# A second layer's up-projections by Strassen's seven block products, with weight operands kept in DRAM

## The chip, the cores and the metric

The program runs on one core of one Trainium2 chip. The metric is device time in microseconds, the median of several executions. TensorE (PE) multiplies matrices into PSUM, VectorE (DVE), ScalarE (ACT) and GpSimd (POOL) work element by element, and SyncE (SP) issues most DMAs. Weights are held as float32r pairs: a high part and a low part, so that one exact product needs three matmuls.

## The reference, cut to what matters

Linear attention is followed by two gated layers on 2304 tokens (4 batches of 576). The weights and q, k, v arrive as 64-bit floats.

```
x = attention(q, k, v)                     # 2304 x 512
g = x @ w_gate;  val = x @ w_val           # 512 -> 1536
x = (g * sigmoid(g) * val) @ w_out         # layer 1, 1536 -> 512
a = x @ w_a;     b = x @ w_b               # layer 2
out = (a * b) @ w_out2
```

## The kernel before, in words

Tokens are in four blocks of 512 (one for each batch) and a rest block of 256 (the last 64 tokens of each batch). `order` runs layer 1 on blocks 0, 1, 2, rest, 3 and then layer 2 on blocks 0 to 3 and the rest. In a block a loop runs over 12 tiles f of 128 hidden columns. `ups` (L739, `up` L757) multiplies both up-projection weights with x: for each matrix 3 precision passes by 4 chunks of the 512 input columns, so 24 matmuls of 128x512 in two PSUM banks (`gv0`, `gv1`). `gated` (L772) forms the gate on ACT, multiplies on DVE and splits the result into a high part (ACT) and a low part (DVE). `down` (L784) multiplies it with the tile's output weights, 12 matmuls into four accumulators `acc0` to `acc3`, one tile behind `ups`.

Weights are converted on the chip. `convert` (L327) loads the 64-bit words through SP (L351, L356), builds a float32 on ACT and DVE (L380 to L401) and splits it (L406, L298) into the tile's buffer `w0` to `w11` in SBUF. Layer 2 uses the same twelve buffers: its tile f is converted when the last block of layer 1 has used that buffer (`convert_tile(1, f)`; the loads are held by `not_before` until that block has begun). The attention of batches 2 and 3 (`attend`, L440) runs beside layer 1 and uses the staging buffers `wr0`, `wr1`, `a0`, `a1` too.

The order of instructions on every engine is made ahead of time by the class `Plan`. Each operation has a cost in microseconds, and some have a due time: `main["at"]` counts the matmuls' time from `FIRST` and adds `BESIDE` per block for attention. Due times run backward along the dependences; `order` (L117) then goes forward and gives each engine the ready operation with the earliest due time. `pair` (L295) may put an operation on VectorE or on GpSimd; `split` (L303) is a high part on ACT and a low part by `pair`. On the chip each engine runs its list in order and waits by semaphores.

Of the kernel before, what the change touches and what calls it, by code (L numbers as in the profile page):

```python
# [30 lines left out]
class Plan:  # L31
# [20 lines left out]
    def add(self, engine, cost, fn, reads=(), writes=(), due=None, after=(), table=None, nbytes=0, other=None,  # L52
            port=None, hold=()):
        n = len(self.ops)
        deps, order, allocs = set(), set(after) | set(hold), []
        for access, write in [(a, False) for a in reads] + [(a, True) for a in writes]:
            buf, part = access if isinstance(access, tuple) else (access, None)
            if not buf.users:
                if isinstance(buf.tag, tuple):
                    allocs.append(buf)  # L60
                else:
                    if buf.tag in self.last:
                        deps.update(self.last[buf.tag].users)
                    else:
                        buf.free = True
                    self.last[buf.tag] = buf
            elif buf.users[0] != n and not buf.free:
                order.add(buf.users[0])
            if not buf.users or buf.users[-1] != n:
                buf.users.append(n)  # L70
            for key, (last, readers) in buf.seen.items():
                if part is None or key is None or key == part:
                    if last is not None:
                        deps.add(last)
                    if write:
# [142 lines left out]
def kernel(  # L218
# [60 lines left out]
    plan = Plan()  # L279
    add = plan.add  # L280

    def act_us(n):
        return 0.18 + n / 1200

    def dve_us(n, rate=1):
        return 0.15 + n / 960 / rate

    def pool_us(n, streams=2):
        return (0, 0.14 + n / 1100, 0.15 + n / 449, 0.18 + n / 590)[streams]
# [5 lines left out]
    def pair(n, out, x, y, op, reads, writes, either=True, port=True):  # L295

        def run(engine):
            engine.tensor_tensor(out=out(), in0=x(), in1=y(), op=op)  # L298

        add("vector", dve_us(n), lambda: run(nc.vector), reads, writes,  # L300
            other=("gpsimd", pool_us(n), lambda: run(nc.gpsimd), True) if either else None, port=port)

    def split(hi, lo, src, n, hi_key, lo_key, src_key, psum=False):  # L303
        add("scalar", act_us(n), lambda: nc.scalar.copy(out=hi(), in_=src()), [src_key], [hi_key])  # L304
        pair(n, lo, src, lambda: hi().bitcast(F32), ALU.subtract, [src_key, hi_key], [lo_key], not psum, not psum)

    def dma(fn, nbytes, reads, writes, due=None, after=(), issue=0.475, queue="sync", hold=()):
        return add(queue, issue, fn, reads, writes, due=due, nbytes=nbytes, after=after, hold=hold)
# [15 lines left out]
    TOP = 122880.0  # L324
# [85 lines left out]
    def convert_tile(l, f):  # L410
        runs, raw = [(h, [0, 1, 2], [h]) for h in range(2)], None
        if l == 0 and f <= AHEAD:
            raw = Buf(wp, [P, 2, 3, WH, 2], U32, f"w{f + NF - KD - AHEAD - 1}", f"wr{l}_{f}")
            list(convert(l, f, runs, raw))
        else:
            for run in runs:
                list(convert(l, f, [run]))


    def rest(h):  # L420
# [313 lines left out]
    def product(cost, fn, reads, writes):  # L734
        n = add("tensor", cost, fn, reads, writes, due=main["at"], after=main["last"])
        main["at"] += cost
        main["last"] = (n,)
# [63 lines left out]
    def finish(l, i, acc):  # L801
        n = widths[i]
        m = n if l == 0 else DM
        for o, ps in enumerate(acc):
            ob = Buf(op, [P, 512], F32, ("ob0", "ob1"), f"ob{l}_{i}_{o}")

            def copy(engine, fn, us, cols, ob=ob, ps=ps):
                add(engine, us(m), lambda: fn(out=ob()[:, cols], in_=ps()[:, cols]), [ps], [(ob, cols.start)])  # L808

            if (l, i) == (1, B):  # L810
                copy("scalar", nc.scalar.copy, act_us, slice(0, m // 2))
                copy("vector", nc.vector.tensor_copy, dve_us, slice(m // 2, m))
            elif o % 2 == 0:
                copy("scalar", nc.scalar.copy, act_us, slice(0, m))
            else:
                copy("vector", nc.vector.tensor_copy, dve_us, slice(0, m))
            if l == 0:
                dma(lambda ob=ob, o=o: nc.sync.dma_start(out=xd[1][i]()[:, o, :], in_=ob()[:, 0:n]),
                    P * n * 4, [ob], [(xd[1][i], o)], due=main["at"] + 10)
            else:  # L820
                if i < B:
                    rows = [(slice(0, P), out[i * S:i * S + SM, :].rearrange("(p r) e -> p r e", r=R)[:, o, :])]
                else:
                    nb = P // SL
                    rows = [(slice(h * SL, (h + 1) * SL), out[(o * nb + h) * S + SM:(o * nb + h + 1) * S, :])
                            for h in range(nb)]
                for at, row in rows:
                    dma(lambda ob=ob, at=at, row=row: nc.sync.dma_start(out=row, in_=ob()[at, :]),
                        P * DM * 4 // len(rows), [ob], [], due=main["at"] + 10)


    order = [(0, i) for i in (*range(B - 1), B, B - 1)] + [(1, i) for i in range(B + 1)]
    FIRST = 28.0
    BLOCK = NF * 3 * 3 * KD * SM / 2400 * 1.0625
    BESIDE = 11.0

# [25 lines left out]
            list(attend(1, g, None, FIRST + BLOCK * (g + 0.8) / KD))  # L862
    for b in range(2, B):
        for g in range(KD):
            list(attend(b, g, None, FIRST + (BLOCK + BESIDE) * (b - 1) + BLOCK * (g + 0.4) / KD))

    main["at"] = FIRST
    for j, (l, i) in enumerate(order):
        if (l, i) == (1, 0):
            not_before.extend(begun)  # L870
            for f in range(NF):
                convert_tile(1, f)
        acc = [Buf(pa, [P, 512], F32, f"acc{o}", f"acc{l}_{i}_{o}")
               for o in range(KD if l == 0 else widths[i] // P)]
        x = xhl
        before = None
        for f in range(NF):
            ga, gb = ups(l, i, f, x)
            if (l, i, f) == (0, B - 1, 0):
                begun = main["last"]  # L880
            h = gated(l, i, f, ga, gb)
            if before:
                down(l, i, f - 1, before, acc)
            before = h
            if j < B - 1:
                main["at"] += BESIDE / NF
        if j + 1 < len(order):
            xhl = next_x(*order[j + 1])
        down(l, i, NF - 1, before, acc)
        finish(l, i, acc)  # L890

    with tc.manual_schedule():
        plan.emit()
# [30 lines left out]
```

## Time and profile before

| | us |
|---|---|
| median of 3 runs | 992.24 (991.45 to 992.66) |
| span of the profiled execution | 989.2 |
| its own whole time | not listed on the page |
| PE busy | 955.1 (97%), 4616 matmuls |
| DVE busy | 417.3 (42%) |
| ACT busy | 402.8 (41%) |
| POOL busy | 104.5 (11%) |
| moved by DMA | 74.19 MB, mean 75 GB/s |

The span runs from the first to the last instruction. Layer 1 fills it from about 40 to 538 us, layer 2 from 538 to 984. In the table of groups the duration of a matmul includes its way through the array, which overlaps with the next; the time from one matmul to the next is read from the chain of waits.

### The profile page before, as it was taken

The numbers are of one execution on the slowest core, as the hardware profiler recorded it, in microseconds if no ns is written. First come the engines' busy times: TensorE is split into PE (matmuls) and PEld (weight loads), VectorE is DVE, ScalarE is ACT, GpSimd is POOL, SyncE is SP. The second block draws the span as 40 slices with busy tenths as digits, with TensorE's granted clock in tenths as the row PEclk, the third lists the DMA queues.
The fourth block names the chain that finished last, engine by engine and source line by source line (L and its number), as shares of the span: only waits on it lengthen the run. The fifth ranks groups of instructions, "written<-read, shape, count | busy, mean of one in ns | idle before, by whom it ended". The sixth has DMA issues, their size and how long they took to land.

```text
span 989.2 us, 12151 instructions
## 1 busy us (share of the span) xinstructions
PE 955.1 (97%) x4616; PEld 794.2 (80%) x4616; DVE 417.3 (42%) x708; ACT 402.8 (41%) x780; POOL 104.5 (11%) x158
## 2 busy tenths in 40 slices
PE   4789889999999999999999999999999999999997
PEld 3578678888888888998888888888888888888897
DVE  7998985323333332126777782221122112111211
ACT  4888986544544542125555551211121112111211
POOL 5613211000000000001112220000000000000000
PEclk9999999999999999999999999999999999999999
DMA  9935543111211113015445530200020001000100
GB/s 266 289 93 166 173 137 105 49 48 49 91 45 47 48 49 108 11 48 172 132 128 163 178 96 1 64 21 1 1 67 20 1 1 64 1 1 1 43 1 22
DMA packets 77138, 74.19 MB, mean 75 GB/s; under 512 B 29976, under 2 KB 64280, under 8 KB 76184
## 3 DMA queue, kind: packets, MB, share of 16 engines
q1 hardware_dynamic: 71416, 69.36, 22.8%
q10 hardware_dynamic: 5664, 4.07, 1.3%
q8 instruction: 36, 0.59, 0.3%
q14 instruction: 22, 0.18, 0.1%
HBM read 60.29 MB, written 13.11 MB: 74 GB/s over the span
## 4 chain that ended last, share of the span: by engine, by line
PE 91%; DMA 3%; DVE 2%; ACT 1%; SPq 1%; issue 1%; POOL 0%; DVEq 0%; ACTq 0%; POOLq 0%
PE u L765 58%; PE acc L795 15%; PE acc L792 14%; PE xt L699 1%; PE kv L638 1%; DMA ut<-in_q_dram 1%; DMA wr<-in_moe_w_out_dram 1%; DMA wr<-in_moe_w_gate_dram 1%; DMA wr<-in_moe_w_val_dram 0%; DMA x<-xq 0%; SPq L526 0%; PE qt L686 0%; ACT wr L385 0%; SPq L351 0%; DMA ut<-in_k_dram 0%
## 5 line engine op out<-in xcount | busy, mean ns | idle before, releaser
L765 PE MATMUL u<-xhl,w 128*128 128x512 f32 (+1 forms) x2856 | 618.7, 371 | 3.5 <-DVE h L298 1.6
L765 PEld LDWEIGHTS u<-xhl,w 128*128 128x128 f32 x2856 | 496.2, 188 | 98.0 <-issue 3.4
L779 DVE TENSOR_TENSOR u<-s,u 128x512 f32<-128x512 f32 (+1 forms) x120 | 77.1, 642 | 402.8 <-PE u L765 377.9
L776 ACT ACTIVATE s<-u 128x512 f32<-128x512 f32 (+1 forms) x120 | 66.6, 555 | 270.2 <-PE u L765 269.9
L792 PE MATMUL acc<-h,w 128*128 128x512 f32 (+1 forms) x720 | 164.5, 376 | 1.2 <-DVE ob L808 1.0
L795 PE MATMUL acc<-w,h 128*128 128x512 f32 x648 | 157.4, 392 | 0.0
L792 PEld LDWEIGHTS acc<-h,w 128*128 128x128 f32 x720 | 124.1, 188 | 28.1 <-issue 1.9
L795 PEld LDWEIGHTS acc<-w,h 128*128 128x128 f32 x648 | 120.9, 188 | 25.6
L304 ACT CAST h<-u 128x512 fp32r<-128x512 f32 (+1 forms) x120 | 65.0, 542 | 185.6 <-DVE u L779 182.8
L298 DVE TENSOR_TENSOR h<-u,h 128x512 fp32r<-128x512 f32 (+1 forms) x120 | 76.4, 636 | 52.1 <-ACT h L304 51.9
L396 DVE SCALAR_TENSOR_TENSOR a<-wr,a 128x768 uint32<-128x768 uint32 (+2 forms) x45 | 51.2, 1137 | 0.8
L406 ACT CAST w<-a 128x768 fp32r<-128x768 f32 (+2 forms) x45 | 39.3, 874 | 17.5 <-DVE a L401 13.1
L298 POOL TENSOR_TENSOR xhl<-xraw,xhl 128x512 fp32r<-128x512 f32 (+1 forms) x6 | 7.3, 1219 | 346.4 <-ACT xhl L304 249.6
L385 ACT ACTIVATE wr<-wr 128x768 uint32<-128x768 uint32 (+2 forms) x45 | 43.0, 957 | 1.4 <-DMA wr<-in_moe_w_out_dram 1.4
L776 ACT ACT_TABLE_LOAD x24 | 30.8, 1283 | 30.6 <-PE u L765 30.5
L380 ACT ACTIVATE a<-wr 128x768 f32<-128x768 f32 (+2 forms) x35 | 33.4, 954 | 14.5 <-DMA wr<-in_moe_w_out_dram 8.1
L401 POOL TENSOR_TENSOR a<-a,wr 128x768 uint32<-128x768 uint32 (+1 forms) x12 | 23.0, 1916 | 148.7 <-DVE a L396 106.6
L401 DVE CUSTOM_DVE_ANT_0 a<-wr,a 128x1536 uint16<-128x1536 uint16 (+1 forms) x33 | 34.7, 1052 | 1.7
L298 POOL TENSOR_TENSOR w<-a,w 128x768 fp32r<-128x768 f32 (+1 forms) x13 | 25.9, 1989 | 82.5 <-ACT w L406 82.5
L298 DVE TENSOR_TENSOR w<-a,w 128x768 fp32r<-128x768 f32 (+2 forms) x32 | 33.1, 1044 | 2.8 <-ACT w L406 2.7
L387 DVE TENSOR_SCALAR a<-a 128x768 f32<-128x768 f32 (+2 forms) x45 | 28.5, 634 | 6.0 <-ACT a L380 5.6
L390 DVE TENSOR_SCALAR a<-a 128x768 uint32<-128x768 uint32 (+2 forms) x45 | 26.7, 594 | 0.8
(107 smaller groups left out, 469.8 us busy)
## 6 DMA issues: line engine op xcount, KB each, us to landing
wr<-in_moe_w_out_dram SPq DMA_DIRECT2D x46, 256.0 KB, 3.7
xraw<-x SPq DMA_DIRECT2D x7, 1024.0 KB
wr<-in_moe_w_a_dram SPq DMA_DIRECT2D x24, 256.0 KB, 3.7
wr<-in_moe_w_b_dram SPq DMA_DIRECT2D x24, 256.0 KB, 3.1
wr<-in_moe_w_gate_dram SPq DMA_DIRECT2D x22, 256.0 KB, 5.2
wr<-in_moe_w_val_dram SPq DMA_DIRECT2D x22, 256.0 KB, 4.3
x<-ob SPq DMA_DIRECT2D x16, 256.0 KB, 2.5
out_dram<-ob SPq DMA_DIRECT2D x16, 256.0 KB, 3.6
```

Source lines behind the costliest of these rows:

```text
L298: engine.tensor_tensor(out=out(), in0=x(), in1=y(), op=op)
L304: add("scalar", act_us(n), lambda: nc.scalar.copy(out=hi(), in_=src()), [src_key], [hi_key])
L380: add("scalar", act_us(e) + 0.08, lambda rows=rows, halves=halves: nc.scalar.activation(out=a(halves).bitcast(F32), in_=rows()[..., 1].bit ...
L385: add("scalar", act_us(e) + 0.08, lambda rows=rows: nc.scalar.activation(out=rows()[..., 0], in_=rows()[..., 0], func=AF.Copy, scale=2.0 * ...
L396: add("vector", dve_us(e), lambda rows=rows, halves=halves: nc.vector.scalar_tensor_tensor(out=a(halves), in0=rows()[..., 1], scalar=0xC00 ...
L401: engine.tensor_tensor(out=a(halves), in0=a(halves), in1=rows()[..., 0], op=ALU.add)
L406: add("scalar", act_us(size), lambda: nc.scalar.copy(out=part(0), in_=a().bitcast(F32)), every, his)
L765: nc.tensor.matmul(ps()[:, 0:n], lhsT=wv[:, c, :], rhs=x()[:, xs, c, 0:n], start=(a == 0 and c == 0), stop=(a == 2 and c == KD - 1))
L776: add("scalar", act_us(n), lambda: nc.scalar.activation(out=s()[:, 0:n], in_=ga()[:, 0:n], func=AF.Silu if l == 0 else AF.Copy), [ga], [s] ...
L779: add("vector", dve_us(n), lambda: nc.vector.tensor_tensor(out=gb()[:, 0:n], in0=s()[:, 0:n], in1=gb()[:, 0:n], op=ALU.mult), [s, gb], [gb])
L792: nc.tensor.matmul(ps()[:, 0:n], lhsT=w()[:, 4 + ws, o * P:(o + 1) * P], rhs=h()[:, hs, 0:n], start=begin, stop=end)
L795: nc.tensor.matmul(ps(), lhsT=h()[:, hs, o * P:(o + 1) * P], rhs=w()[:, 4 + ws, :], start=begin, stop=end)
```

## The change

Layer 2 is rewritten for the four full blocks. Two blocks of 512 tokens are taken together (a half), and two tiles f (a pair, 256 hidden columns of each matrix). The product of x (512 input columns by 2 blocks) with a pair is a product of 2 by 2 blocks: the input halves h, the token blocks t and the tiles i. It is done by seven products instead of eight, in Winograd's form: four sums of the weights (`t1` to `t4`), four sums of x (`parts`), and seven sums of products (`begin`, `middle`, `end`). One product, `one(m, o)`, is 6 matmuls for matrix m.

The weights of layer 2 are converted by `convert_pair` during layer 1, after the attention of batch 3 (`pair_buf["after"]`). The eight blocks b11 ... t4 of a pair and its output weights are split and stored in DRAM (`wd`). In layer 2 each of 12 steps (2 halves by 6 pairs) loads seven operands into a ring of nine units of 512 KB (in the freed buffers w5 to w8), the output weights into a double buffer, and in the second half b12 for the rest block.

Products go through four PSUM banks (`gv0`, `gv1`, `at0`, `at1`), three for each matrix. The output is no longer gathered in PSUM over all tiles: each step's 8 (or 10) output chunks of 6 matmuls are added into `SUMS` in SBUF. A step's chunks run at the end of the next step. The rest block is done in the second half's steps (`rest_up`). In the due times of layer 1, attention units now follow each other at `EACH` = 22 us and the blocks have other shares of `BESIDE`.

```diff
 def split(hi, lo, src, n, hi_key, lo_key, src_key, psum=False):
+    src_keys = src_key if isinstance(src_key, list) else [src_key]
 ...
+NP = NF // 2
+wd = [Buf(dp, [P, 10, 1024], F32, f"wd{j}", f"wd{j}") for j in range(NP)]
+def convert_pair(j, m):
+    for i in range(2):
+        ...
+        dma(get, P * 2 * WH * 8, [], [LOW, HIGH], issue=0.95 if m < 2 else 0.475, after=pair_buf["after"])
+        ... # abs, scale, clamp, shift, merge, add: 512 columns each
+    def keep(i, h, to):
+        ...
+        split(hi, lo, lambda: a(i)[:, h], WH, ...)
+        ...
+        dma(put, P * 2 * WH * 4, [(key[0], ("s", 0)), (key[0], ("s", 1))], [(wd[j], ...)])
+    if m < 2:
+        ... # keep 4 blocks, 4 subtractions of 256 columns, keep 4 sums
+    else:
+        ... # keep 4 blocks
 ...
-order = [(0, i) for i in (*range(B - 1), B, B - 1)] + [(1, i) for i in range(B + 1)]
+order = [(0, i) for i in (*range(B - 1), B, B - 1)]
+EACH = 22.0
 ...
-        list(attend(b, g, None, FIRST + (BLOCK + BESIDE) * (b - 1) + BLOCK * (g + 0.4) / KD))
+        before = len(plan.ops)
+        list(attend(b, g, None, FIRST + BLOCK + BESIDE + EACH * ((b - 2) * KD + g + 0.4)))
+pair_buf["after"] = tuple(range(before, len(plan.ops)))
 ...
-    if (l, i) == (1, 0):
-        not_before.extend(begun)
-        for f in range(NF):
-            convert_tile(1, f)
 ...
+        if (j, f) == (1, 0):
+            ...
+            for n in range(NP):
+                for m in range(3):
+                    convert_pair(n, m)
 ...
-        if j < B - 1:
-            main["at"] += BESIDE / NF
+        main["at"] += (BESIDE, 2 * BESIDE, BESIDE, 5, 0)[j] / NF
 ...
+PART = 1024
+RING = 9
+BANKS = ("gv0", "gv1", "at0", "at1")
+blocks = [(0, 1), (2, 3)]
+def parts(s):
+    ... # load the halves of two blocks: RAW[0..3]; halve = split of 1024 columns
+    halve(0, 0)
+    halve(5, 3)
+    less(3, 2, 3, ALU.add)
+    less(2, 0, 2)
+    less(0, 3, 0)
+    halve(1, 0)
+    halve(2, 3)
+    halve(3, 1)
+    less(1, 1, 0)
+    halve(4, 2)
+    halve(6, 1)
+def step(s, j):
+    n = s * NP + j
+    w = [unit(14 + (7 * n + o) % RING) for o in range(7)]
+    wo = outs_w[n % 2]
+    for o in range(7):
+        get_w(w[o], j, o)
+    for i in range(2):
+        get_w(wo[i], j, 8 + i)
+    if s:
+        get_w(b12, j, 7)
+    def one(m, o, ps, first):
+        ...
+            for a, (ws, xs) in enumerate(((1, 0), (0, 1), (0, 0))):
+                for c in range(2):
+                    nc.tensor.matmul(ps(), lhsT=wv(o)[:, m, ws, c, :], rhs=..., start=first and a == 0 and c == 0, ...)
+    def begin(m):
+        one(m, 0, p[m][0], True)
+        copy(t[0], p[m][0])
+    def middle(m):
+        one(m, 1, p[m][1], True)
+        plus(t[1], p[m][1], t[0])
+        one(m, 2, p[m][2], True)
+        one(m, 3, p[m][0], False)
+        if m == 0:
+            copy(A[3], p[m][0])
+        else:
+            plus(A[3], p[m][0], A[3], ALU.mult)
+            later.append(lambda: halve(0, 0, A[3]))
+        one(m, 4, p[m][1], False)
+        plus(t[2], p[m][1], t[0])
+        plus(t[2], p[m][2], t[2])
+        if m:
+            times(t[2], A[2])
+            later.append(lambda: halve(1, 1, t[2]))
+    def end(m, which):
+        ... # which 0: product 5 into p[m][1], then t[0]; which 1: product 6 into p[m][2], then t[1]
+    def rest_up(i):
+        ... # 2 x 12 matmuls of 256 columns, gate, split later
+    def out_chunk(k):
+        ... # 6 matmuls of 512 columns into acc{k % 4}, then SUMS[k] += (copy for the first pair)
 ...
+for s in range(2):
+    parts(s)
+    if s:
+        rest_parts()
+    for j in range(NP):
+        begin, middle, end, rest_up, chunks = step(s, j)
+        begin(0)
+        middle(0)
+        begin(1)
+        end(0, 0)
+        end(0, 1)
+        middle(1)
+        for which in range(2):
+            if left:
+                left.pop(0)()
+            end(1, which)
+        for i in range(2 * s):
+            rest_up(i)
+        for c in left:
+            c()
+        for halve in later:
+            halve()
+        later.clear()
+        left = chunks
+    if s == 0:
+        for c in left[:-2]:
+            c()
+        left = left[-2:]
+for c in left:
+    c()
```

## Rows read from the trace of the kernel before

**Rows 1.** Cores: span and mean granted TensorE clock.
```profile
core 0: 989.2 us, clock 0.996
```
**Rows 2.** Page, chain that ended last: shares of the span by engine.
```profile
PE 91%; DMA 3%; DVE 2%; ACT 1%; SPq 1%; issue 1%; POOL 0%; DVEq 0%; ACTq 0%; POOLq 0%
```
**Rows 3.** Stretches: rest block and block 3 of layer 1, a layer 2 block.
```profile
core 0: us, PE busy (x) PEld busy (x) DVE busy (x) ACT busy (x) POOL busy (x), PEclk, DMA share, GB/s
...
386.00:437.00 51.00, 50.00 (x418) 49.46 (x417) 10.54 (x25) 9.61 (x25) 0.00 (x0) 1.00 0.13 42
437.00:538.00 101.00, 100.83 (x451) 82.68 (x450) 72.40 (x102) 55.98 (x81) 14.28 (x8) 1.00 0.45 141
...
637.00:735.30 98.30, 98.30 (x434) 81.16 (x433) 19.95 (x29) 17.47 (x30) 1.30 (x1) 1.00 0.06 22
```
**Rows 4.** Chain pieces in layer 2: start us, us, what.
```profile
735.31 10.88 PE u L765 x48
746.19 2.75 PE acc L795 x12
...
978.03 2.88 PE u L765 x24
```
**Rows 5.** Groups by shape: busy us, mean ns, idle before and releaser.
```profile
L779 DVE TENSOR_TENSOR u<-s,u 128x512 f32<-128x512 f32 x96 | 66.8, 696 | 335.6 <-PE u L765 310.7 <-issue 15.8 <-PE kb L580 4.9
...
L298 DVE TENSOR_TENSOR xhl<-xraw,xhl 128x512 fp32r<-128x512 f32 x23 | 15.6, 716 | 1.0 <-ACT xhl L304 1.0
...
L298 POOL TENSOR_TENSOR xhl<-xraw,xhl 128x512 fp32r<-128x512 f32 x5 | 6.5, 1298 | 249.6 <-ACT xhl L304 249.6
...
L298 DVE TENSOR_TENSOR w<-a,w 128x768 fp32r<-128x768 f32 x27 | 25.5, 952 | 2.8 <-ACT w L406 2.7
...
L298 DVE TENSOR_TENSOR h<-u,h 128x256 fp32r<-128x256 f32 x24 | 10.2, 424 | 10.1 <-ACT h L304 10.1
```
**Rows 6.** PE's waits, whole span: us in total, times, longest.
```profile
PE acc L792 <- DVE ob L808: 1.0, 1, 1.0
```
**Rows 7.** Groups by shape: VectorE's conversion instructions of 768 columns.
```profile
L387 DVE TENSOR_SCALAR a<-a 128x768 f32<-128x768 f32 x38 | 22.9, 603 | 5.9 <-ACT a L380 5.6
L390 DVE TENSOR_SCALAR a<-a 128x768 uint32<-128x768 uint32 x38 | 21.1, 556 | 0.7
L396 DVE SCALAR_TENSOR_TENSOR a<-wr,a 128x768 uint32<-128x768 uint32 x38 | 41.6, 1096 | 0.7
L401 DVE CUSTOM_DVE_ANT_0 a<-wr,a 128x1536 uint16<-128x1536 uint16 x29 | 27.7, 955 | 1.7
```
**Rows 8.** Timeline of PE: the last attention unit's output matmuls.
```profile
380.25 1.02 PE L699 MATMUL xt<-uc 128*128 128x512 f32 x2
```
**Rows 9.** SP's own waits: us in total, times, longest.
```profile
SPq L725 <- DVE xhl L298: 229.3, 3, 89.3
```
**Rows 10.** DMA: issues to landing; GB/s in 40 slices of 437 to 448.
```profile
wr<-in_moe_w_a_dram SPq DMA_DIRECT2D x24, 256.0 KB, 3.7
...
GB/s 0 0 0 0 0 0 0 0 60 0 0 160 291 15 11 216 257 4 298 179 60 179 477 268 209 298 328 298 328 387 320 365 257 384 387 372 395 384 376 387
```
**Rows 11.** Chain pieces at the end of the span.
```profile
983.71 0.38 ACT ob L808
...
984.11 0.42 DVE ob L808
```
**Rows 12.** Timeline of PE in layer 1's first block.
```profile
55.63 2.10 PE L638 MATMUL kv<-ut 128*128 128x130 f32 x8 [2.49 <-ACT ut L616]
```
**Rows 13.** PE's waits between 100 and 150 us.
```profile
PE kv L638 <- ACT ut L616: 1.7, 1, 1.7
```
**Rows 14.** Stretches: the granted clock (PEclk) around and after waits.
```profile
100.00:150.00 50.00, 44.48 (x208) 35.43 (x207) 43.86 (x75) 43.24 (x83) 11.74 (x13) 1.00 0.52 164
...
54.00:57.00 3.00, 1.37 (x6) 1.37 (x7) 3.00 (x5) 3.00 (x4) 0.00 (x0) 0.72 0.44 100
57.00:60.00 3.00, 3.00 (x14) 2.62 (x13) 3.00 (x6) 3.00 (x4) 2.62 (x2) 0.71 0.02 4
```

More of the change, by code (lines that the diff above doesn't have):

```diff
@@ L303, in split @@
     def split(hi, lo, src, n, hi_key, lo_key, src_key, psum=False):
-        add("scalar", act_us(n), lambda: nc.scalar.copy(out=hi(), in_=src()), [src_key], [hi_key])
-        pair(n, lo, src, lambda: hi().bitcast(F32), ALU.subtract, [src_key, hi_key], [lo_key], not psum, not psum)
+        src_keys = src_key if isinstance(src_key, list) else [src_key]
+        add("scalar", act_us(n), lambda: nc.scalar.copy(out=hi(), in_=src()), src_keys, [hi_key])
+        pair(n, lo, src, lambda: hi().bitcast(F32), ALU.subtract, [*src_keys, hi_key], [lo_key], not psum, not psum)
     def dma(fn, nbytes, reads, writes, due=None, after=(), issue=0.475, queue="sync", hold=()):
@@ L878 @@
             ga, gb = ups(l, i, f, x)
-            if (l, i, f) == (0, B - 1, 0):
-                begun = main["last"]
+            if (j, f) == (1, 0):
+                pair_buf["bits"] = [Buf(sp, [P, 1536], U32, (t,), f"pair{t}") for t in WR]
+                pair_buf["a0"], pair_buf["a1"] = [Buf(sp, [P, n], U32, (t,), f"pair{t}") for t, n in zip(AT, (1536, 768))]
+                pair_buf["first"] = len(plan.ops)
+                for n in range(NP):
+                    for m in range(3):
+                        convert_pair(n, m)
+                pair_buf["first"] = tuple(range(pair_buf["first"], pair_buf["first"] + 20))
             h = gated(l, i, f, ga, gb)
@@ L890, with unit @@
         finish(l, i, acc)
+    PART = 1024
+    RING = 9
+    halves = [Buf(wp, [P, 3, PART], F32R, f"w{n}", f"l2w{n}") for n in range(1, NF - 1)]
+    def unit(u):
+        return (halves[u // 3], u % 3), lambda: halves[u // 3]()[:, u % 3, :]
+    ops_x = [[unit(2 * o + t) for t in range(2)] for o in range(7)]
+    rest_h = unit(23)
+    hs2_w = [unit(24 + t) for t in range(2)]
+    outs_w = [[unit(26 + 2 * n + i) for i in range(2)] for n in range(2)]
+    last = [Buf(wp, [P, 3, PART], F32, "w0", "raw2"), Buf(wp, [P, 3, PART], F32R, "w0", "rest2")]
@@ new lines @@
+    b12 = (last[1], 0), lambda: last[1]()[:, 0]
+    rest_x = [((last[1], 1 + t), lambda t=t: last[1]()[:, 1 + t]) for t in range(2)]
+    raws = [Buf(sp, [P, 2, PART], F32, ("xraw",), "r1")]
+    late = [Buf(sp, [P, 1536], F32, (t,), f"r2{t}") for t in WR]
+    RAW1 = [((raws[0], 0), lambda: raws[0]()[:, 0]), ((raws[0], 1), lambda: raws[0]()[:, 1])]
+    RAW2 = [[((last[0], x), lambda x=x: last[0]()[:, x]) for x in range(2)],
+            [((late[x], 0), lambda x=x: late[x]()[:, 0:PART]) for x in range(2)]]
@@ new lines @@
+    temps = Buf(wp, [P, 6, 512], F32, f"w{NF - 1}", "temps")
+    tc_ = Buf(hp, [P, 512], F32, ("s",), "tc")
+    tr = Buf(hp, [P, 2 * P], F32, ("tm",), "tr")
+    T = [[((temps, n), lambda n=n: temps()[:, n]) for n in range(3)] + [((tc_, 0), lambda: tc_())],
+         [((temps, n), lambda n=n: temps()[:, n]) for n in range(3, 6)]]
+    rest_s = ((tr, 0), lambda: tr())
+    h1 = [Buf(hp, [P, 2, 512], F32R, (f"h{t}",), f"hp{t}") for t in range(2)]
+    hs2 = [[((h1[t], 0), lambda t=t: h1[t]().rearrange("p s n -> p (s n)")) for t in range(2)],
+           hs2_w]
@@ new lines, with bank, halve, less @@
+    sums = Buf(xp, [P, 2 * R, 512], F32, "xhl", "sums")
+    rest_sums = [Buf(op, [P, 512], F32, (f"ob{n}",), f"rs{n}") for n in range(2)]
+    SUMS = [((sums, k), lambda k=k: sums()[:, k]) for k in range(2 * R)] + \
+        [((b, 0), lambda b=b: b()) for b in rest_sums]
+    BANKS = ("gv0", "gv1", "at0", "at1")
+    blocks = [(0, 1), (2, 3)]
+    def bank(name):
+        return Buf(pg, [P, 512], F32, BANKS, name)
+    def parts(s):
+        RAW = [*RAW1, *RAW2[s]]
+        for q, (t, h) in enumerate(((0, 0), (0, 1), (1, 0), (1, 1))):
+            i = blocks[s][t]
+            last_x[:] = [dma(lambda q=q, i=i, h=h: nc.sync.dma_start(
+                out=RAW[q][1]().rearrange("p (c n) -> p c n", c=2), in_=xd[1][i]()[:, 2 * h:2 * h + 2, :]),
+                P * PART * 4, [xd[1][i]], [RAW[q][0]],
+                after=[*last_x, *(pair_buf["first"] if s else ())])]
+        def halve(o, q):
+            (hi_key, hi), (lo_key, lo) = ops_x[o]
+            split(hi, lo, RAW[q][1], PART, hi_key, lo_key, RAW[q][0])
+        def less(q, x, y, op=ALU.subtract):
+            pair(PART, RAW[q][1], RAW[x][1], RAW[y][1], op, [RAW[x][0], RAW[y][0]], [RAW[q][0]])
+        halve(0, 0)
[9 more added lines that the diff above has]
+        halve(6, 1)
@@ new lines, in rest_parts, with get_w @@
+    def rest_parts():
+        last_x[:] = [dma(lambda: nc.sync.dma_start(
+            out=RAW1[0][1]().rearrange("p (c n) -> p c n", c=KD), in_=xd[1][B]()),
+            P * PART * 4, [xd[1][B]], [RAW1[0][0]], after=last_x)]
+        (hi_key, hi), (lo_key, lo) = rest_x
+        split(hi, lo, RAW1[0][1], PART, hi_key, lo_key, RAW1[0][0])
+    def get_w(to, j, o, n=1):
+        keys = [(wd[j], (o, m)) for m in range(2)]
+        dma(lambda: nc.sync.dma_start(out=to[1]().bitcast(F32), in_=wd[j]()[:, o, :]), P * PART * 4, keys, [to[0]])
@@ new lines @@
+    left, later = [], []
+    for s in range(2):
[26 more added lines that the diff above has]
+            left = left[-2:]
```

154 lines of the change are left out of this document (added).

## The prediction

> **What bounds the kernel now.** I read the views from the coarse to the fine. The cores view gives one core, a span of 989.2 us and a mean TensorE clock of 0.996 [rows 1]: there is no time to win from the clock. The chain of waits is 91% TensorE and only 3% DMA [rows 2]. The stretches then say where TensorE is full: in a 98.3 us block of the second layer (637.0 to 735.3) PE is busy for all 98.3, VectorE for 20.0 and DMA for 6% of its share; in the first layer's last block, with weight conversions beside it, PE is busy 100.8 of 101.0 and VectorE 72.4 [rows 3]. So the second layer costs exactly what its matmuls cost, and what they cost is read from the chain inside one block: 48 up-projection matmuls in 10.88 us, which is 226.7 ns each, and 12 down-projection matmuls in 2.75 us, 229 ns [rows 4]. The check: a block has 288 of the first and 144 of the second, 65.3 + 33.0 = 98.3 us, the measured stretch. In the mean durations of the group table matmuls overlap, so those are not used.
>
> **What it removes.** For two blocks and two f tiles the old program issues 2 x 2 x 24 = 96 up-projection matmuls of 512 columns. The new step issues 7 products x 2 matrices x 6 = 84. Over 2 halves x 6 pairs that is 1008 for 1152; the down-projections (12 x 48 + 72 = 648) and the rest block's 288 matmuls of 256 columns (24 in 2.88 us, 120 ns each [rows 4]) stay in number and shape. 144 x 226.7 ns = 32.6 us leave TensorE. The Trainium skill (TensorE: Matmul & The Clock Gate, section Back-to-back issue gap) would price a warm 512-column matmul at 512/2.4 + 2.5 = 215.8 ns; by that the gain would be 31.1 us and the time 1.5 us longer. The row is 5% above the rule, and the row is used.
>
> A step then lasts 84 x 226.7 + 48 x 229 ns = 30.0 us in the first half, and in the second, with 12 more down and 48 rest matmuls, 30.0 + 2.7 + 5.8 = 38.5 us. One product or one output chunk is 6 matmuls, about 1.37 us; I call this a slot.
>
> **VectorE beside a step.** A step has 11 adds or multiplies that read a product from PSUM and 8 that add an output chunk, 19 x 0.696 = 13.2 us by the 512-column row; 3 multiplies and 4 low-part subtractions in SBUF at 0.716 make 5.0 more [rows 5]. 18.2 of 30.0 us is 61% of VectorE, where today a block uses 20%; GpSimd may take the last seven at 1.30 each. TensorE sees this only where a bank is to be reused. Four banks serve six products, and the shortest way round is that of product 4 to product 5 of the same matrix: between them stands one slot, 1.37 us, in which VectorE must read the bank, 0.70. Spare: 0.67. It happens twice a step. One strange instruction just started in front (0.70) eats that spare and no more; two in front cost about 0.7. Bounds 0 and 24 x 0.7 = 17 us; I take 0.5, near the lower end, because TensorE's waits for VectorE on a bank today come to one of 1.0 us [rows 6]. In the very first step no output chunk stands in that place: the full 0.70 and its hand-over are waited for, 0.8 us.
>
> **The change of half.** All operands of x sit in one set of buffers. The block that the first chain of sums starts from (A22) may be split only when product 5 of the old half has read its predecessor; the second product of the new half stands behind it through three sums. From there TensorE still has 14 slots (19.2 us) before the new step and 7 products (9.5 us) before the last operand is wanted. In that time VectorE has 11 instructions of 1024 columns, an estimate of 1.19 each from 0.716 at 512 and 0.952 at 768 [rows 5], 13.1 us; 13 chunk adds, 9.0; and 8 others, 5.6: 27.7 us. If nothing goes to GpSimd and the operands come last, TensorE waits 27.7 - 19.2 = 8.5 us; if GpSimd takes a third, nothing. I take 1.5.
>
> **The start of the layer.** The first x operands need weight buffers 1 to 5 of the first layer, free some 55 us into its last block, so 40 us remain for the same 13.1 us of VectorE work, which is 72% busy there today with conversions [rows 3]. 0 to 3 us; I take 0.5.
>
> **Conversions moved.** Per pair of f tiles VectorE has, by the 768-column rows cut to 512 (two thirds of 0.603, 0.556, 1.096 and 0.955, 2.1 us) [rows 7], 6 x 2.1 = 12.8 us, and 28 subtractions of 256 columns at 0.424 [rows 5], 11.9: 24.7 us. The order lets them begin when the attention of the last batch has been issued. Its last unit is due at 329.0 in the old program's due times and at 299.7 in the new; on the chip its last large matmul stands at 380.25 [rows 8], so I put the new one at 345. After that VectorE is 20% busy (10.5 of 51.0 us [rows 3]), so a pair takes 31 us if VectorE is the limit, and I allow 40 for hand-overs: the sixth pair is done at about 585. The first is wanted at 538, the sixth at 538 + 19 + 4 x 30 = 677. They cost nothing up to (677 - 345)/6 = 55 us a pair.
> What they can hold up is the first layer's gating. In its full blocks the last block today shows the same mixture at 0.2 us of idle PE. The rest block (386 to 437) today has no conversions and only 1.4 us of down-projection to cover the gating; one conversion instruction in front (1.096 x 2/3 = 0.73) in each of 12 tiles would be 8.8 us, none 0. I take 0.5. A gain from this part ends at the 1.0 us that PE idles there now.
> Each pair also issues 6 loads and 20 stores on SP. A store waits for its low part, and behind it in that queue stand later loads, among them the next block's x; today SP waits only until that load's buffer is free, 229.3 us in three waits [rows 9], so the load leaves nearly a block ahead of its use and a delay of some microseconds is covered.
>
> **The stream.** A step of the first half fetches 9 operands of 512 KB, 4.72 MB in 30.0 us, 157 GB/s; one of the second 10, 5.24 MB in 38.5 us. A 256 KB load lands 3.7 us after its issue, and with several in flight the queue moves up to 380 GB/s [rows 10]. Two of the ring's nine units are always a step ahead; the others are freed by the second matrix's product and wanted some 17 slots (23 us) later. One load alone would be 3.7 + 0.26 MB at 380 = 4.4 us. So it is hidden, 0; the other bound, strictly one load after another, is the second rival.
>
> **The end.** Today an ACT copy (0.38) and a VectorE copy (0.42) follow the last matmul [rows 11]; then one add of 0.70 does. 0.
>
> **The sum.** Span 989.2 - 32.6 + 0.8 + 0.5 + 1.5 + 0.5 + 0.5 = 960.4. What lies around the span I take as the median less the span, 992.24 - 989.2 = 3.0, because the page gives the profiled execution no other time; it may be off by the 1.2 us over which the runs spread. 963 us, 2.9% less. With low ends and the 1.0 us gained it is 958; 970 takes in a part of the upper ends.
>
> **Rivals.**
> 1. The wait moves into the bank rotation: VectorE's order puts two instructions ahead at most of the 24 places, and the change of half costs its upper end. For it: VectorE goes from 20% to 61%, and its order is fixed beforehand. Against: the one 1.0 us wait of its kind today. 963 + 16 + 7 = 986 at worst, 978 in the middle.
> 2. Slower: the in-order SP queue serves the weight stream one load after another, because a load that waits for its unit holds those behind it. At 4.4 us a load the steps last 39.6 and 44 us for 30.0 and 38.5, 6 x 9.6 + 6 x 5.5 = 91 us more, 1054. It begins to cost at 3.3 us a load and passes the old time when 114 loads take the matmuls' 411 us and 29 more, 3.9 us a load. Against it: bursts of 380 GB/s with several in flight.
> 3. The conversions come too late: above 55 us a pair every microsecond costs six, from 60 on the old time is passed; at 65, 1023 us. Against it: 24.7 us of VectorE work.
> 4. The clock falls in the second layer. Today a wait of 2.49 us stands ahead of a stretch granted 0.72 and 0.71 of full speed; 0.56 and 0.58 of those two 3 us stretches at the lower level (1.2 GHz) is 3.4 us, half of it lost: 1.7 us. Between 100 and 150, with 5.5 us idle in waits of at most 1.7, the clock stayed at 1.00 [rows 12 to 14]. Were each of 12 steps to wait 2.5 us and lose 1.7, 1013. The Trainium skill (TensorE: Matmul & The Clock Gate, section A second HAM failure mode: psum-queue depth-cycling) says that cycling through PSUM banks leaves small idles after which the clock falls back again and again, which is what these four banks do. By that rule the fall comes without the long wait, 963 + 12 x 1.7 = 983; the stretch from 100 to 150 speaks against it.
> That it does not remove the matmuls is not open: the loops can be counted.
>
> **Chances.** Forecast (958 to 970): 0.68. Rival 1 (970 to 988): 0.15. Rival 2: 0.07. Rival 3: 0.03. Rival 4: 0.02. Something unnamed: 0.05. Less than 0.2% (2 us) is what a measurement of this kernel cannot tell from no change. Faster: 0.68 + 0.15 and 0.03 of the others, 0.86; same: 0.03 of the unnamed and mild forms; slower: 0.07, 0.03 and 0.01, so 0.11. The range 958 to 986 holds the forecast and nearly all of rival 1 and leaves 0.18 outside.
>
> **What would show it.** Right: up-projection matmuls of the second layer at 1008 + 288, about 227 ns apart, PE idle below 1 us in a step, stores of weights ending before 600. Wrong: a wait of PE for VectorE in every step (rival 1), for a weight operand's DMA in most (2), for it only in the first half with stores still running (3), or a granted clock below 1.00 after 540 (4).

## The result: 963.0 us, 2.9% less

| | before | after |
|---|---|---|
| median of 4 runs, us | 991.97 (991.45 to 992.66) | 963.01 (962.07 to 965.87) |
| ratio | | 0.9713 [0.9699, 0.9728] |
| profiled execution, us | | 963.11, span 961.3 |
| matmuls | 4616 | 4472 |
| layer 2, first to last matmul, us | 538.81 to 983.68: 444.9 | 539.10 to 956.72: 417.6 |
| after the last matmul, us | 5.5 | 4.6 |

The median is the predicted one. Not every term behind it is: one was nearly three times too small, and others that were too large made up for it. The views of after show both.

The cores view of after answers to [rows 1]:

```profile
core 0: 961.3 us, clock 0.992
```

The clock is lower by 0.004, which looks like nothing. About half of that is lost in layer 1, around 140 us (rows in the last section), and half in layer 2, where the stretches show it. From the page, the shares of the chain by engine, as in [rows 2]:

```profile
PE 90%; DVE 4%; ACT 3%; DMA 2%; issue 1%; POOL 0%; SPq 0%; ACTq 0%; POOLq 0%; DVEq 0%
```

TensorE is still the bound, but VectorE's share has doubled: on the chain stand a few waits that were not there. Stretches of layer 2 in after, with the columns of [rows 3]:

```profile
core 0: us, PE busy (x) PEld busy (x) DVE busy (x) ACT busy (x) POOL busy (x), PEclk, DMA share, GB/s
539.10:557.00 17.90, 17.12 (x76) 13.85 (x75) 10.88 (x19) 5.98 (x12) 6.73 (x8) 1.00 0.99 326
557.00:690.00 133.00, 133.00 (x587) 109.91 (x586) 90.75 (x151) 48.16 (x96) 53.02 (x52) 1.00 0.82 284
690.00:740.00 50.00, 47.52 (x201) 38.33 (x200) 36.06 (x44) 11.92 (x15) 13.15 (x7) 0.97 0.50 161
715.00:718.00 3.00, 0.79 (x3) 0.51 (x3) 3.00 (x4) 0.00 (x0) 1.12 (x1) 0.94 0.00 0
718.00:721.00 3.00, 3.00 (x9) 2.35 (x8) 3.00 (x4) 0.00 (x0) 0.00 (x0) 0.50 1.01 335
721.00:724.00 3.00, 3.00 (x14) 2.45 (x14) 1.62 (x3) 0.57 (x2) 0.00 (x0) 0.99 0.53 140
740.00:950.00 210.00, 209.90 (x1058) 178.59 (x1057) 100.73 (x155) 36.68 (x72) 18.06 (x14) 1.00 0.37 122
```

Read it by the missing time. From 557 to 690 PE is busy for all 133.0 us, beside VectorE at 68%, conversions still running and DMA at 0.82 of its share; from 740 to 950 it lacks 0.1. What is lost stands at the first step (0.8) and between 690 and 740 (2.5), where the halves change; in layer 2 the clock falls there alone, to 0.50, the lower level, from 718 to 721.

Pieces of the chain in after answer to [rows 4]:

```profile
555.48 0.70 DVE temps L298
...
556.23 19.38 PE p L1089 x84
...
589.28 16.32 PE p L1089 x72
...
611.06 8.20 PE o L1184 x36
...
695.28 1.23 DVE l2w L298
696.51 0.61 DVE temps L298
697.12 0.04 issue
697.16 1.65 PE p L1089 x6
...
717.42 4.59 PE o L1184 x12
722.01 16.45 PE p L1089 x72
...
743.91 5.75 PE q L1158 x48
...
771.83 5.75 PE q L1158 x48
777.58 11.07 PE o L1184 x48
```

16.32 us for 72 product matmuls are 226.7 ns each, 8.20 for 36 output matmuls 227.8, 5.75 for 48 of the rest block 119.8: the durations that the prediction carried over. 1008, 648 and 288 of them make 228.5 + 147.6 + 34.5 = 410.6 us of the 417.6, so 7.0 are waits, and matmuls that took longer than these. The first step has 0.77 of wait and 0.3 in the piece behind it (84 x 226.7 ns = 19.04, it took 19.38). The place at 697 has 0.28 of wait and 0.3 (1.65 for 1.36). The change of half has the wait below and 4.59 us for 12 matmuls that are worth 2.73. Together these are 5.7 of the 7.0 us; the rest is spread over the layer in small pieces. PE's waits after 530 us, as in [rows 6] (in us: total, times, longest):

```profile
PE o L1184 <- DVE sums L298: 2.2, 1, 2.2
PE p L1089 <- DVE temps L298: 1.1, 2, 0.8
```

Three waits in the whole layer. The largest is not on a product's bank but on an output chunk's: VectorE was late adding chunks into `SUMS`. Why, its timeline shows (after; start, us, instruction):

```profile
704.92 1.47 DVE L298 TENSOR_TENSOR temps<-temps 128x512 f32<-128x512 f32 x1
706.32 0.68 DVE L298 TENSOR_TENSOR sums<-o,sums 128x512 f32<-128x512 f32 x1
707.14 2.08 DVE L298 TENSOR_TENSOR l2w<-temps,l2w 128x512 fp32r<-128x512 f32 x1
...
712.67 1.21 DVE L298 TENSOR_TENSOR r<-r2wr,r 128x1024 f32<-128x1024 f32 x1
713.81 2.86 DVE L298 TENSOR_TENSOR hp<-temps,hp 128x512 fp32r<-128x512 f32 x1
716.59 2.47 DVE L298 TENSOR_TENSOR sums<-o,sums 128x512 f32<-128x512 f32 x4
```

and GpSimd's in the same time:

```profile
704.54 1.30 POOL L298 TENSOR_TENSOR hp<-tc,hp 128x512 fp32r<-128x512 f32 x1
705.80 2.87 POOL L298 TENSOR_TENSOR l2w<-r2wr,l2w 128x1024 fp32r<-128x1024 f32 x1
713.31 2.81 POOL L298 TENSOR_TENSOR l2w<-r2wr,l2w 128x1024 fp32r<-128x1024 f32 x1 [4.64 <-ACT l2w L305]
```

Put them side by side. GpSimd's instructions end at 705.84, 708.67 and 716.12; VectorE's stretched ones end at 706.39, 709.22 and 716.67, 0.55 us later each time. A VectorE instruction with both operands in SBUF, worth 0.69, did its work only when GpSimd was through. `sums<-o,sums` at 706.32, with one operand in PSUM, took its 0.68 beside the same GpSimd instruction. The last of the three carries the wait: had `hp<-temps,hp` taken 0.68 instead of 2.86, the chunk adds behind it would have begun 2.2 us earlier, and 2.2 us is what TensorE waited for them.

### The profile page after: what moved, and what is told of

Same layout as the page of the kernel before. It is cut to its first block, busy times and chain, and to the rows that moved or that the text cites. A ratio compares the mean times of both kernels' runs of the same rounds, so it can differ in the third digit from the quotient of the medians.

```text
span 961.3 us, 13055 instructions
## 1 busy us (share of the span) xinstructions
PE 927.6 (96%) x4472; PEld 769.0 (80%) x4472; DVE 567.3 (59%) x988; ACT 426.8 (44%) x884; POOL 219.3 (23%) x282
## 4 chain that ended last, share of the span: by engine, by line
PE 90%; DVE 4%; ACT 3%; DMA 2%; issue 1%; POOL 0%; SPq 0%; ACTq 0%; POOLq 0%; DVEq 0%
PE u L856 29%; PE p L1089 24%; PE acc L883 15%; PE o L1184 14%; PE q L1158 4%; PE kv L729 1%; PE xt L790 1%; PE qt L777 1%; DMA x<-xq 1%; DMA rests<-in_q_dram 1%; DVE l2w L298 0%; ACT w L407 0%; ACT L714 0%; DVE ut L298 0%; ACT ut L714 0%
## 5 line engine op out<-in xcount | busy, mean ns | idle before, releaser
L856 PE MATMUL u<-xhl,w 128*128 128x512 f32 (+1 forms) x1416 | 316.5, 376 | 3.4 <-DVE h L298 1.5
L856 PEld LDWEIGHTS u<-xhl,w 128*128 128x128 f32 x1416 | 244.3, 189 | 53.2 <-issue 4.4
L1089 PE MATMUL p<-l2w,l2w 128*128 128x512 f32 x996 | 232.0, 390 | 1.2 <-DVE temps L298 1.1
L1089 PEld LDWEIGHTS p<-l2w,l2w 128*128 128x128 f32 x996 | 186.6, 188 | 41.3 <-DVE temps L298 1.9
L298 DVE TENSOR_TENSOR temps<-p,temps 128x512 f32<-128x512 f32 x120 | 82.9, 691 | 85.3 <-PE p L1089 80.1
L1184 PE MATMUL o<-l2w,l2w 128*128 128x512 f32 x360 | 98.4, 392 | 0.0
L1184 PE MATMUL o<-l2w,hp 128*128 128x512 f32 x288 | 82.9, 397 | 2.2 <-DVE sums L298 2.2
L1184 PEld LDWEIGHTS o<-l2w,l2w 128*128 128x128 f32 x360 | 68.2, 189 | 15.1
L298 DVE TENSOR_TENSOR sums<-o,sums 128x512 f32<-128x512 f32 x80 | 54.6, 689 | 33.4 <-PE o L1184 32.6
L1184 PEld LDWEIGHTS o<-l2w,hp 128*128 128x128 f32 x288 | 54.3, 190 | 14.1 <-issue 2.6
L473 POOL TENSOR_TENSOR paira<-paira,pairwr 128x512 uint32<-128x512 uint32 x18 | 24.7, 1375 | 65.6 <-DVE paira L468 26.8
```

Source lines behind the costliest of these rows:

```text
L473: engine.tensor_tensor(out=u32(i), in0=u32(i), in1=r(i)[..., 0], op=ALU.add)
L856: nc.tensor.matmul(ps()[:, 0:n], lhsT=wv[:, c, :], rhs=x()[:, xs, c, 0:n], start=(a == 0 and c == 0), stop=(a == 2 and c == KD - 1))
L1089: nc.tensor.matmul(ps(), lhsT=wv(o)[:, m, ws, c, :], rhs=ops_x[o][xs][1]().rearrange("p (c n) -> p c n", c=2)[:, c, :], start=first and a ...
L1184: nc.tensor.matmul(ps(), lhsT=lhs(i, hs), rhs=wo[i][1]()[:, ws * 512:(ws + 1) * 512], start=i == 0 and a == 0, stop=i == 1 and a == 2)
```

## The experiments

Each is timed against the kernel before, on one chip with it. That kernel took 991.74 us beside the runs with one product more, one sum in a spare buffer, layer 2 without GpSimd and one pair of conversions, and 992.27 beside the others.

**One product more.** Each step issues the first product of each matrix twice: the old number of matmuls in the new order.

```diff
         one(m, 0, p[m][0], True)
+        one(m, 0, p[m][0], True)
         copy(t[0], p[m][0])
```

> The first product of each matrix in each step is issued twice (the second starts its bank afresh, so nothing else changes): 144 matmuls of 512 columns are back, as many as the old program had. Theory (the gain is the matmuls, the rest of the rewriting costs some 6 us): 963.0 + 144 x 0.2267 = 995.6 us, slower than the old program by about 4, and the wait in the very first step stays. Rival (part of the gain is elsewhere, or the extra slot absorbs waits of the new program): 985 to 992.

990.74 us, ratio 0.999 [0.9981, 0.9999], span 988.7. Its waits after 530 us:

```profile
PE p L1089 <- DVE temps L298: 1.1, 2, 0.8
```

The matmuls put back are worth 32.6 us and cost 27.4 of span (988.7 - 961.3). The difference is mostly the change of half, whose wait is gone, as the rival had it with its 985 to 992. VectorE is still stretched there (2.07 us beside a GpSimd instruction of 2.89), but TensorE no longer waits for it; that the extra product gives VectorE the time it lacked is the likely reason and was not tried by itself. With the old number of matmuls nothing of the gain is left, so the gain is their number; the theory's 995.6 was off by the wait that these matmuls hide.

**One sum into a spare buffer.** At the change of half A21 + A22 goes into `a0`'s space, so that the first sum no longer waits for product 5 of the old half; product 5's own operand is split last.

```diff
 ...
+        if s:
+            RAW.append(((extra, 0), lambda: extra()[:, 0:PART]))
+            halve(0, 0)
+            less(4, 2, 3, ALU.add)
+            less(2, 0, 2)
+            less(0, 4, 0)
 ...
+            halve(6, 1)
+            halve(5, 3)
```

> At the change of half the sum A21+A22 goes into a spare buffer instead of over A22, so that the chain of sums no longer begins behind the split of A22, which must wait for product 5 of the old half. The same 11 instructions of 1024 columns stay. Theory (the order, not the amount, makes the wait): sums start as soon as the x blocks are loaded, the wait of PE for VectorE at the change (2.2 us, and 1.9 us of matmul time at the lower clock behind it) goes, 958.5 us. Rival (27.7 us of VectorE work in 19.2 us, however ordered): the wait stays above 1.5 us, 962 to 963.

958.93 us, 0.9667 [0.9653, 0.968], span 957.1. Its waits after 530 us:

```profile
PE p L1104 <- DVE temps L298: 1.6, 2, 0.9
```

The wait at the change of half is gone; those on a product's bank rose from 1.1 to 1.6. An earlier start cures it, as expected. GpSimd still has its long instructions here, and one of VectorE's took 2.89 us beside one of 2.90 and ended 0.54 behind it, but nothing waited for it. By itself this run does not tell whether VectorE had too much to do or was held up.

**Layer 2 without GpSimd.** Every `pair` of layer 2 goes to VectorE.

```diff
+    both = pair
+    def pair(n, out, x, y, op, reads, writes, either=True, port=True):
+        both(n, out, x, y, op, reads, writes, False, port)
```

> In the second layer every elementwise pair runs on VectorE, none on GpSimd (the conversions still may use it). Theory of the prediction (27.7 us of VectorE work at the change of half and GpSimd takes a part): with all of it on VectorE the wait at the change grows to 8.5 us, with the low clock behind it 968 to 970 us. Rival (GpSimd's long instructions hold VectorE up: a VectorE subtraction of 512 columns took 2.78 us beside one of GpSimd of 2.81): taking them away frees as much as it adds, 961 to 964 us, and no VectorE row of 512 columns above 0.8 us in the layer after the conversions.

959.38 us, 0.9675 [0.9662, 0.9688], span 957.3. The prediction's reason, that GpSimd lightens VectorE here, falls. VectorE at the change of half in this kernel:

```profile
711.39 1.21 DVE L298 TENSOR_TENSOR r<-r2wr,r 128x1024 f32<-128x1024 f32 x1
712.52 0.68 DVE L298 TENSOR_TENSOR l2w<-temps,l2w 128x512 fp32r<-128x512 f32 x1
713.13 0.68 DVE L298 TENSOR_TENSOR hp<-temps,hp 128x512 fp32r<-128x512 f32 x1
```

The same `hp<-temps,hp` takes 0.68 where it took 2.86, and the stretch from 690 to 740:

```profile
690.00:740.00 50.00, 49.73 (x221) 40.82 (x220) 40.53 (x56) 12.88 (x17) 0.00 (x0) 1.00 0.57 178
```

VectorE has 40.5 us of work in it, 4.5 more than in after, and TensorE waits 0.3 instead of 2.5. The prediction's bound for just this case, everything on VectorE, was a wait of 8.5 us. It put all 11 instructions of 1024 columns into the 19.2 us ahead of the new step. In this kernel seven lie there; two were done before, and two come after the step's first product at 717.98. From 699 to 717.7 VectorE was busy 17.7 of 18.7 us, which fits.

**Only the long instructions away from GpSimd.** In `parts` (1024 columns) VectorE alone; the 512-column ones may still go to GpSimd.

```diff
 ...
+    def pair(n, out, x, y, op, reads, writes, either=True, port=True):
+        both(n, out, x, y, op, reads, writes, either and not (alone[0] and n == PART), port)
+    alone[0] = True
     def parts(s):
```

> Only the 1024-column sums and subtractions on x are kept from GpSimd; its 512-column instructions stay. Theory (it is GpSimd's long instructions, 2.4 to 2.9 us each, that hold VectorE's up at the change of half): 959 to 959.5 us, as with none on GpSimd. Rival (GpSimd's short ones do as much, or the order that came with the other kernel did it): 961 to 963.

959.09 us, 0.9671 [0.9656, 0.9685], span 956.7. Its waits after 530 us:

```profile
PE p L1097 <- DVE temps L298: 1.1, 2, 0.8
```

This one edit takes the whole loss away: the few GpSimd instructions of 2.4 to 2.9 us at the change of half were its cause. The order that `Plan` makes is a new one in this kernel too, so the run alone leaves the order as a rival; against it stand the 2.2 us worked out above inside one trace. GpSimd's instructions of 512 columns, 1.3 us, delay VectorE too (`temps` at 704.92 in after), but TensorE's waits for VectorE are here the same 1.1 us in two as without GpSimd, so they cost nothing that shows.

**One pair of conversions.** Only the first pair of tiles is converted, and all steps read its operands; the conversion of the other five is left out.

```diff
-                for n in range(NP):
+                for n in range(1):
 ...
-        ... in_=wd[j]()[:, o, :]
+        ... in_=wd[0]()[:, o, :]
```

> Only the first pair of tiles is converted; all steps read its operands from DRAM, with the same stream (the output is that of one pair used six times). Left out: five sixths of the conversions, their loads and stores. Theory (the conversions are hidden beside the matmuls): 962 to 963 us, PE's waits as before within 0.5 us. Rival (they hold the second layer up while DMA is 80 to 90% busy, from 540 to 690): 958 to 960 us, with the gain between 540 and 720.

962.78 us, 0.9711 [0.9697, 0.9724]. Its stretch from 540 to 690 and its waits:

```profile
540.00:690.00 150.00, 149.22 (x658) 123.03 (x657) 73.28 (x108) 28.22 (x48) 15.85 (x12) 1.00 0.53 173
```

```profile
PE o L1184 <- DVE sums L298: 2.2, 1, 2.2
PE p L1089 <- DVE temps L298: 1.1, 2, 0.8
```

In that stretch 28 us of VectorE's work and 43 of GpSimd's are gone (101.6 and 58.9 in after) with a third of the DMA, and TensorE's time and waits are the same. Where they stand in after, the conversions are free.

**The conversions 40 us later.** They are released only by the matmuls of a later block.

```diff
-            if (j, f) == (1, 0):
+            if (j, f) == (3, 0):
+                pair_buf["after"] = (*pair_buf["after"], *main["last"])
```

> The conversions of the second layer's weights may begin only with the first layer's rest block, some 40 us later than in the changed kernel (about 386 instead of 345 us). There the first pair took 44 us and the last ones 66, and the last operand of the sixth pair was stored at 661, about 12 us before its load had to leave. Theory (VectorE, SP and DMA give no faster pace beside the stream): the whole delay arrives, less the 12 us: 988 to 992 us, with waits of PE for weight operands in the first half. Rival (the slow pace of the last pairs is the order's choice, since they are not due earlier): the pairs close up, 963 to 968 us.

991.57 us, 0.999 [0.9979, 1.0001]: the whole gain is lost. The first load goes out at 389.2 (345.7 in after), the last store at 702.2 (672.3). Its waits of PE after 530 us:

```profile
PE p L1090 <- DMA l2w<-wd: 20.9, 4, 11.3
PE o L1185 <- DVE sums L298: 2.9, 2, 2.1
PE p L1090 <- DVE temps L298: 1.7, 3, 0.8
```

and two of its stretches:

```profile
700.00:720.00 20.00, 11.53 (x42) 9.34 (x43) 3.64 (x6) 2.20 (x4) 0.00 (x0) 0.69 0.80 273
720.00:740.00 20.00, 19.73 (x87) 15.95 (x86) 14.92 (x19) 4.73 (x6) 9.04 (x5) 1.00 0.51 164
```

Of the 28.1 us of span that it loses to after (989.4 - 961.3), 20.9 are waits for operands, of which after has none. Behind them the clock is lower (0.69 from 700 to 720); the 60 product matmuls after the longest wait took 15.80 us where 13.60 were due. The third rival's cliff is there; after stands short of it. How short: its last store of products' operands and the load behind it go out at 661.4 and 661.9, the five loads are issued by 667.0, and the step that reads them starts at 679.2. That is about 12 us; what the loads take to land comes off it, and operands that are used later in the step have more. The late kernel gives nearly the same: its last such store went out at 693.1, 31.7 us later, and 20.9 were waited for, so about 11 were covered. The expected 988 to 992 was met by another sum than the expected one: of 43.5 us of delay at the first load 30 were left at the last store.

**Seven ring units instead of nine.** No unit is a step ahead.

```diff
-    RING = 9
+    RING = 7
```

> The ring of weight operands has seven units instead of nine, so no operand of the next step can be fetched before the product that frees its unit. Theory (17 slots, 23 us, lie between freeing and need, a load takes about 5): 963 us, within 1. Rival (the stream arrives just in time, the two spare units carry it): PE waits for a weight operand in most steps, 970 us and more.

967.22 us, 0.975 [0.9734, 0.9765], span 964.1: neither the theory's "no change" nor the rival's. TensorE waits for the stream once:

```profile
752.63 7.73 PE L1089 MATMUL p<-l2w,l2w 128*128 128x512 f32 x33 [2.78 <-DMA l2w<-wd]
```

and the chain before it names why:

```profile
744.10 2.66 PE q L1158 x23
746.77 5.73 DMA l2w<-wd
```

In the second half the rest block's matmuls read the units as well, so a unit comes free later, and this load landed 5.73 us after that. All other steps run on seven units without a wait. Why only this one was not tried; what differs is that in the later steps of that half 48 output matmuls, 11.07 us, stand between the rest block's and the next step's (at 777.58 in after); and behind the half's first step none. The 2.8 us are the span's difference (964.1 - 961.3); the medians differ by 4.2, but the two kernels were not timed side by side.

**All cures together.** The spare buffer, layer 2 without GpSimd, and in the first step product 4 ahead of product 3 for the second matrix, which gives the bank of the 0.77 us wait a slot more.

```diff
 ...
+            first = m == 1 and n == 0
+            if not first:
+                three()
             one(m, 4, p[m][1], False)
 ...
+            if first:
+                three()
```

> Together: the sum A21+A22 in a spare buffer, all elementwise pairs of the second layer on VectorE, and in the very first step product 4 of the second matrix ahead of product 3, so that a product stands between 4 and 5. Theory: no wait at the change of half (4.4 us less than the changed kernel's) and none in the first step (1.1 us with the slower matmuls behind it): 957.5 us. Rival (the two cures of the change of half cost each other something, or VectorE alone is too slow for both): 959 or more.

956.47 us, 0.9641 [0.9627, 0.9655], span 954.5. Pieces of its chain:

```profile
538.56 35.38 PE p L1109 x156
...
949.91 0.02 issue
949.93 0.69 DVE rs L298
```

After 530 us PE has no wait at all. Layer 2 lasts from 538.56 to 949.91, 411.35 us, where its matmuls alone are worth 410.6. It is the best version found; this layer now costs its matmuls and 0.8 us more.

## Why the prediction was right, step by step

| us of span | predicted | measured |
|---|---|---|
| first layer's gating and the start of layer 2 | +1.0 | +0.3 (539.10 against 538.81) |
| layer 2: -32.6 + 0.8 + 0.5 + 1.5 | -29.8 | -27.3 |
| after the last matmul | 0 | -0.9 |
| span | 960.4 | 961.3 |
| around the span | 3.0 | 1.8 (963.11 - 961.3) |

**The matmuls** are the gain, by number and by duration; the first experiment puts them back and the gain is gone. The Trainium skill (TensorE: Matmul & The Clock Gate, section Back-to-back issue gap) gives 215.8 ns for an isolated one, by its formula, and about 131 for a stream of weight loads and matmuls. This trace again has 226.7, which agrees with neither.

**Before layer 2** the prediction put down 1.0 us, and 0.3 is a sum of opposite parts. The rest block's gating cost nothing: PE is busy 50.98 of the 51.0 us from 386 to 437, so the 1.0 us of idle that stood there is gone. The start of the layer has no wait. On the other side the clock fell around 140 us, as it had not in before.

**The first step** was right: 0.77 for 0.8, with 0.3 more in the matmuls behind the wait.

**The 24 bank places** were right in kind: one strange instruction in front eats the spare, more cost the difference. Of the 24 one failed, at 697, where a single long one (1.23 us) stood in front. With the slower matmuls behind it, it cost 0.6 where 0.5 was put down.

**The change of half** is the term that was mis-sized: 1.5 predicted, about 4.1 measured. 2.2 are the wait, and 1.9 are 12 matmuls at the lower clock (4.59 - 2.73). Three steps of its working failed. It took GpSimd's share as help: "if GpSimd takes a third, nothing". GpSimd did take three of the 1024-column instructions, and that is what made VectorE late; without it, all on VectorE, the wait is gone. VectorE's sum of work was not the limit, and so the bound of 8.5 us fell too, for the case that it was made for. And the price of a wait of 2 us was known from [rows 12, 14], as rival 4, and not added to the wait that the sum itself held. The Trainium skill (SBUF — State Buffer, section Who interferes with whom) has the rule that the prediction did not weigh: a VectorE instruction with two SBUF inputs contends with a GpSimd one that reads SBUF. The three ends 0.55 us behind GpSimd's agree with it; that the instruction with one operand in PSUM was not delayed fits it as well.

**The conversions** cost nothing, as predicted, but on a thinner margin than the text had. The start was right (345.7 for 345), though the due times that the prediction names give 351. The pace was not: from first load to first load 40 to 44 us for the first three pairs, then 58 and 74, and 66 for the last one, 54 on average with the last store at 672, where 40 and 585 were predicted and 55 was the limit. VectorE's 24.7 us a pair [rows 5, 7] did not set it. What did is not settled; in after SP waited at the stores' line for 69 us (42.8 for VectorE, 26.4 for GpSimd), and beside layer 2 DMA was at 0.82 of its share. A pair's loads are ten (60 for six pairs on the page), not the 6 of the prediction.

**The stream** is hidden, as predicted; the second rival's serial queue did not occur, with 284 GB/s through 557 to 690 and no wait for an operand. The ring's two units ahead are needed in one place.

**The end and the time around the span** were two small errors with one sign: 0.9 us less after the last matmul, and 1.8 us around the span where the median of other executions had been used for 3.0. All later profiles lie between 1.8 and 2.2 there. Together with the 0.7 before layer 2 they make up for the 2.5 us by which layer 2 fell short of its forecast, so that the agreement of 963.0 with 963.0 is luck by about 2 us; the range did not need it.

**The rivals.** 1 came in its second half only, the change of half; in the steps the rotation had its slack. 2 did not come. 3 did not, by about 11 us. 4 came once in layer 2, behind the one wait over 2 us, at 1.9 us where the prediction had 1.7 for it. Of the prediction's own signs, one of being wrong came with it, a granted clock below 1.00 after 540, and two of being right did not: PE idle below 1 us in a step, and stores ending before 600. The other form of 4 did not come: beside the four banks in rotation the clock stays at 1.00 through 557 to 690 and 740 to 950. The Trainium skill (TensorE: Matmul & The Clock Gate, section A second HAM failure mode: psum-queue depth-cycling) lays the fall to small idles of TensorE between groups of matmuls. In these two stretches the trace shows next to none, 0.0 of 133 us and 0.1 of 210, so here the rotation brought neither the idles nor the fall. [rows 14] were a weak argument against 4, though: the same part of layer 1 did fall in after.

## What to carry to other kernels

Where TensorE is full, count its matmuls and take their spacing from the chain: that gave the gain to the microsecond (with every wait removed layer 2 is 33.5 us shorter than before, and 32.6 were counted). Before work is put on GpSimd to unload VectorE, look at what VectorE does beside it: an instruction of GpSimd can hold up one of VectorE with both operands in SBUF for most of its own length (here 2.2 of 2.8 us), and it is the longest that breaks the slack. Write down for each covered step how much cover is left; here it was about 11 us of the 333 between the first conversion and the last one's use, and 40 us of delay cost the whole gain.

## What the runs showed of the hardware that was not expected

- A VectorE instruction of 512 columns with both operands in SBUF took 0.68 us alone and 2.08 to 2.86 beside a GpSimd instruction of 2.8 to 2.9; each time it ended 0.55 us after GpSimd's. It goes the other way too: GpSimd's instructions of 1024 columns took 2.41 with none of these beside it (702.18 in after), and 2.81 and 2.87 where a VectorE instruction of this kind was under way as they started.
- Behind a wait of 0.28 or 0.77 us, and in the kernel with late conversions behind one of 2.14, with the clock at 1.00, the next matmuls took 0.3 us more than their spacing, so a short wait costs more than it shows. Why was not tried.
- A wait of 2.2 us left the granted clock at 0.50 for the 3 us after it (718 to 721), which nearly doubled the wait's price. But the length of a wait alone does not tell whether the clock falls. Around 140 us, in layer 1, before and after have the same two waits one behind the other, 1.46 and 1.14 us. In before the clock stayed at 1.00 and the two matmuls behind them took 1.13 us:

```profile
142.40 1.13 PE L699 MATMUL xt<-ut 128*128 128x512 f32 x2 [1.14 <-ACT ut L693]
```

In after it was 0.69 from 140 to 142 and 0.50 from 142 to 144, and they took 2.08:

```profile
140.94 2.08 PE L790 MATMUL xt<-ut 128*128 128x512 f32 x2 [1.14 <-ACT ut L784]
```

And where the conversions came 40 us later, a wait of 2.14 us at the change of half left the clock at 1.00; the 12 matmuls behind it took 3.01 us, where they took 4.59 in after:

```profile
747.47 0.94 PE L1185 MATMUL o<-l2w,hp 128*128 128x512 f32 x3 [2.14 <-DVE sums L298]
```

The 2.78 us with seven ring units left it at 1.00 as well. What decides between the two was not tried.
